# Attention by single tiles against attention by steps of two tiles: transposes and scores in groups, AV products in two places per unit

## The chip, the cores and the metric

The kernel runs on one core of a Trainium2 chip. The metric is the device time of one execution in microseconds; before the change three runs gave 1063.75, 1064.16 and 1065.99, so a median of 1064.16. A profiled execution of the same kernel is where all durations come from.

## The reference

Three stages follow each other. The first is attention over q, k, v of 4 batches x 8 heads x 576 positions x 64, with a bias per head made by a small network from the distance of two positions:

```python
scores = scale * np.matmul(q, k.transpose(0, 1, 3, 2))
scores = scores + bias.transpose(2, 0, 1)[None, :, :, :]
scores = scores - np.max(scores, axis=-1, keepdims=True)
attn = np.exp(scores)
attn = attn / (np.sum(attn, axis=-1, keepdims=True) + 1e-09)
return np.matmul(attn, v)
```

The result, as 2304 tokens of 512, goes through a dense layer with a rational activation (512 to 2048 and back), and then through one of eight experts per token (512 to 1024 and back). The change lies in attention and at its seam to the dense layer.

## The kernel before, in words

**The engines.** TensorE (PE) runs all products and transposes, and writes PSUM. VectorE (DVE), ScalarE (ACT) and GpSimd (POOL) run elementwise work, and SyncE (SP) issues nearly all DMAs. Each engine takes its instructions in the order in which the Python program emits them; the schedule is written out by hand. A tile of a pool with `bufs=2` has two buffers taken in turn: the first write of a new tile waits until the readers of the tile that had its buffer are done.

**Units and tiles.** A unit is one batch and one pair of heads: 16 units, `NU`. Each has nine tiles of 128 rows of scores: eight of one head each (tile t < 4 of the first head, 4 to 7 of the second), and a ninth with the last 64 rows of both heads. `ORD` is the order in which they come: head one and head two in turn, then the ninth.

**What a tile goes through.** `scores(g)` (L330): four fp32r products of 128x288 (eight for the ninth tile) into a PSUM tile `sc` of two banks, of which there are two. `rowmax(g)` (L346, VectorE): adds the bias, writes `e`, takes the row minimum of the negative. `expo(g)` (L351, ScalarE): the exponential with the row sum. `recip` (L363, L364 on VectorE, L366 on POOL): reciprocals of the sums of two tiles, spread into `rb`. `trans_pe` (L393): four transposes of `e` into a one-bank PSUM tile `tr`; after every second tile two more (L396, L397) of the last 64 columns and of `rb` into `rem`, an `av` tile. `trans_evac` (L370, ScalarE): copies 512 columns to `aT`, and after four tiles 512 columns of `rem` to `aR`. `rest_pe`, `rest_evac` (L417, L418) do the same for the ninth tile.

**AV.** `av_pe(u, n, c)` (L436) multiplies by V with 64 stationary columns for each of two heads, for query columns 0 to 255 (n = 0) or 256 to 575 (n = 1), chunk c of five; `av_evac` (L445, VectorE) scales into `xs`, and SP stores `xs` to `xT` (L447). A place in this text is an unbroken stretch of AV products on TensorE.

**Beside it, for later.** For the next unit q and k chunks are transposed into stacks: `stack_pe(u, i)` for i = 0 to 4 (L289, L291, L293, L294), into a `tr` tile, and read by `stack_evac` one loop turn later: for i = 1 and 3 by two VectorE passes (L310, L311), for 0 and 2 by ScalarE (L307), for 4 by two VectorE passes (L302, L303) and then ScalarE's `qrem` (L305). `split_q` (POOL) splits q into two parts. `conv(i, part)` converts the dense layer's weights, 32 pieces, two per unit: part 0 loads (L51, L53), 1 (L61, L62), 3 (L67), 4 (L70) and 5 (L76) are VectorE, 2 is ScalarE's Square (L65), 6 and 8 POOL, 7 stores.

**The order.** The loop `for g in range(NG + 6)` (L524) takes one tile g per turn: exponentials of g - 2, what is pending from the last turn, transposes of g - 4 (`LAG`), scores of g, stack transposes, row maximum of g - 1, AV products of the previous unit. The tables say in which of a unit's nine turns j the rest comes:

```python
CONV = {0: [(6, -1), (8, -1), (1, 0), (2, 0)], 1: [(3, 0), (7, -1), (0, 1)], 2: [(4, 0)], 3: [(5, 0)], 4: [(6, 0)],
        5: [(1, 1), (8, 0)], 6: [(7, 0), (3, 1), (2, 1), (0, 2)], 7: [(4, 1)], 8: [(5, 1)]}
STACK = {0: 4, 1: 0, 2: 1, 3: 2, 7: 3}
SPLIT = {6: (0,), 7: (1,), 8: (2, 3)}
AV0 = {0: (0, 1), 1: (2,), 2: (3, 4)}
AV1 = {4: (0, 1), 6: (2,), 7: (3,), 8: (4,)}
```

**The seam.** `first_x`, `first_split` and `first_mm` (L449 to L477) run the first three chunks of the dense layer's first product (L671) among the last turns of attention, and `Rational` its activation. The dense layer's second product (L759) needs the weights `w_b`, loaded by `load_wo` (L688), which SP issues after the last `xT` store.

**PSUM.** Eight banks: two `sc` tiles of two banks, two `tr` and two `av` of one.

Of the kernel before, what the change touches and what calls it, by code (L numbers as in the profile page):

```python
# [22 lines left out]
P = 128  # L23
# [65 lines left out]
def attention(ctx, tc, k, ins):  # L89
# [115 lines left out]
    NG = 9 * NU  # L205
    ORD = (0, 4, 1, 5, 2, 6, 3, 7, 8)
    LAG = 4
# [72 lines left out]
    def stack_pe(u, i):  # L280
# [3 lines left out]
        ps = pst.tile([P, 512], F32, name="tr")  # L284
# [73 lines left out]
    def recip(g):  # L358

        n = 1 if g % 9 == 8 else 2  # L360
        if g % 9 % 2 or n == 1:
            st = tiles[g][4]
            nc.vector.tensor_scalar(st[:, 2, 0:n], st[:, 1, 0:n], 1e-9, None, ALU.add)  # L363
            nc.vector.reciprocal(st[:, 3, 0:n], st[:, 2, 0:n])  # L364
            rb = recips[g] = ap.tile([P, 2, D], F32, name="rb")
            nc.gpsimd.tensor_scalar(rb, st[:, 3, 0:n].unsqueeze(2).to_broadcast([P, 2, D]), 1.0, 1.0, ALU.mult, ALU.mult)  # L366
# [8 lines left out]
    def trans_pe(g):  # L375
        u, j = divmod(g, 9)
        t = ORD[j]
        r = units[u]
        both = tiles[g][3]
        if j == 0:  # L380
            r.aT = [None, None]
            r.aR = [None, None]
            r.rem = [None, None]
        if j in (0, 4):
            w = Q1 if j == 0 else S - Q1
            n = j // 4
            r.aT[n] = ap.tile([P, 2, 4, w], F32, name=f"aT{n}", bufs=1)
            r.aR[n] = ap.tile([P, 2, w], F32, name=f"aR{n}", bufs=1)
            r.rem[n] = pst.tile([P, 512], F32, name="av")
        ps = r.tps = pst.tile([P, 512], F32, name="tr")  # L390
        for c in range(4):
            e0 = c // 2 * 2 * P + (640 if 4 <= t < 8 else 0)
            nc.tensor.transpose(ps[:, c * P:(c + 1) * P], both[:, e0 + c % 2:e0 + 2 * P:2], k.idf)  # L393
        if j % 2:
            n, q0 = t % 4 // 2, t % 2 * P
            nc.tensor.transpose(r.rem[n][:, Q1 + q0:Q1 + q0 + P], both[:, 512:640], k.idf)  # L396
            nc.tensor.transpose(r.rem[n][:, q0:q0 + P], recips.pop(g).rearrange("p a n -> p (a n)"), k.idf)  # L397

    def trans_evac(g):
        u, j = divmod(g, 9)  # L400
        t = ORD[j]
        r = units[u]
        pv = r.tps.rearrange("p (c n) -> p c n", c=4)
        if t < 8:
            hd, n, q0 = t // 4, t % 4 // 2, t % 2 * P
            evac("A", r.aT[n][:, hd, :, q0:q0 + P], pv)
            if j in (3, 7):
                evac("A", r.aR[n][:, :, 0:Q1], r.rem[n].rearrange("p (a n) -> p a n", a=2))
        else:
            evac("A", r.aT[1][:, :, :, Q1:Q1 + 64], r.tps.rearrange("p (c h n) -> p h c n", c=4, h=2))  # L410
        if t < 8:
            tiles.pop(g)

    def rest_pe(g):
        both = tiles.pop(g)[3]
        av0, rb = units[g // 9].av0, recips.pop(g)
        nc.tensor.transpose(av0[:, 384:512], both[:, 512:640], k.idf)  # L417
        nc.tensor.transpose(av0[:, 256:384], rb.rearrange("p a n -> p (a n)"), k.idf)  # L418

    def rest_evac(g):  # L420
        r = units[g // 9]
        for hd in range(2):
            ls = slice(64 * hd, 64 * hd + 64)
            evac("A", r.aR[1][ls, :, Q1:Q1 + 64], r.av0[ls, 256:512].rearrange("p (a n) -> p a n", a=2)[:, :, 64 * hd:64 * hd + 64])

    def av_pe(u, n, c):
        r = units[u]
        w = Q1 if n == 0 else S - Q1
        if c == 0:
            r.av = pst.tile([P, 512], F32, name="av")  # L430
            if n == 0:
                r.av0 = r.av
# [53 lines left out]
    for s in range(37):  # L486
        if s == 24:
            conv(0, 0)
# [1068 lines left out]
```

## Time and profile before

| | before |
|---|---|
| runs | 1063.75, 1064.16, 1065.99 us (median 1064.16) |
| the profiled execution's own time | 1065.21 us |
| its span | 1063.4 us |
| TensorE busy, products / weight loads | 1018.1 us (96%) / 885.9 us (83%) |
| VectorE busy | 749.7 us (70%) |
| ScalarE busy | 650.2 us (61%) |
| POOL busy | 277.0 us (26%) |

The span is the time from the first to the last instruction of the profiled execution. Busy shares are means over stages: until about 63 us the bias is made, until about 397 us attention runs, then the dense layer and the experts. A row of a timeline has start, duration, engine, line of the kernel, operation, tiles as out<-in, shapes and a count of merged instructions; in brackets the idle time of the engine before it and what ended it. On TensorE instructions overlap, so the time that one takes from the others is read from start to start.

### The profile page before, as it was taken

What the parts mean: (1) busy time and instruction counts of PE and PEld (TensorE: products, weight loads), DVE (VectorE), ACT (ScalarE), POOL (GpSimd) and SP (SyncE); (2) the same over time, 40 slices, a digit from 0 to 9 for tenths busy, and PEclk for the clock granted to TensorE, in tenths of its full rate; (3) what the DMA queues carried; (4) which work ended last, traced back from release to release, by engine and by line L of the source; (5) the groups of instructions that cost most, each with busy time, mean ns of one, the idle gap of its engine ahead of it and who ended that gap; (6) DMA issues with size and microseconds to landing.
All of it is one profiled execution on the core that took longest, in us unless ns stands there. A gap on an engine that the chain in (4) does not pass through costs nothing. (4 is left out here: it accounts for less than half of the span.)

```text
span 1063.4 us, 19125 instructions
## 1 busy us (share of the span) xinstructions
PE 1018.1 (96%) x6804; PEld 885.9 (83%) x6804; DVE 749.7 (70%) x1544; ACT 650.2 (61%) x1283; POOL 277.0 (26%) x449
## 2 busy tenths in 40 slices
PE   6889999999999999999999999999997899999995
PEld 4667777777777779999999999999996789999983
DVE  7988898888888858888888988988885412111210
ACT  6878788888878856676667666666664322222221
POOL 3434344343343310202103012021041533211210
PEclk9999999999999999999999999999998999999998
DMA  5885885784664327005103121051240356411100
GB/s 166 290 277 159 235 250 171 214 236 118 189 185 116 99 74 296 30 1 23 38 1 31 30 21 40 1 30 60 81 80 1 24 159 215 141 42 40 51 31 18
DMA packets 122072, 113.34 MB, mean 107 GB/s; under 512 B 65055, under 2 KB 94495, under 8 KB 121952
## 3 DMA queue, kind: packets, MB, share of 16 engines
q1 hardware_dynamic: 117828, 101.53, 35.8%
q0 software_dynamic: 3728, 10.25, 3.2%
q8 instruction: 61, 1.00, 0.4%
q14 instruction: 59, 0.48, 0.2%
q10 hardware_dynamic: 396, 0.08, 0.0%
HBM read 78.09 MB, written 33.79 MB: 105 GB/s over the span
## 5 line engine op out<-in xcount | busy, mean ns | idle before, releaser
L759 PE MATMUL sc<-gh,w_b 128*128 128x384 f32 x752 | 208.8, 339 | 1.3 <-ACT x L766 1.3
L759 PEld LDWEIGHTS sc<-gh,w_b 128*128 128x128 f32 x752 | 138.6, 189 | 2.2 <-ACT x L766 1.9
L759 PE MATMUL sc<-gl,w_b 128*128 128x384 f32 x376 | 127.1, 338 | 0.0
L393 PEld LDWEIGHTS tr<-idf,e 128*128 128x128 f32 x576 | 80.5, 207 | 49.2 <-issue 25.0
L351 ACT ACTIVATE e<-e,st 128x576 f32<-128x576 f32 x144 | 112.2, 779 | 12.2 <-DVE st L346 10.3
L370 ACT COPY aT<-tr 128x512 f32<-128x512 f32 x144 | 84.5, 587 | 45.8 <-PE tr L393 44.0
L346 DVE CUSTOM_DVE_ANT_0 e<-sc,bias_s 128x576 f32<-128x576 f32 x144 | 107.7, 749 | 5.1 <-PE sc L330 4.0
L1086 DVE SCALAR_TENSOR_TENSOR hl<-tr,hh 128x256 fp32r<-128x256 f32 x56 | 23.8, 425 | 121.4 <-ACT hh L1085 119.5
L671 PE MATMUL tr<-kn,w_a 128*128 128x384 f32 x372 | 107.1, 342 | 0.1
L393 PE MATMUL tr<-idf,e 128*128 128x128 f32 x576 | 104.6, 304 | 1.7 <-DVE kk L311 0.9
L330 PE MATMUL sc<-kk,qS 128*128 128x288 f32 x512 | 99.1, 315 | 0.7 <-DVE st L346 0.7
L660 ACT CAST gh<-t 128x768 fp32r<-128x768 f32 x47 | 39.3, 836 | 86.2 <-DVE t L656 86.2
L436 PE MATMUL av<-aT,vn 128*64 128x320 f32 (+1 forms) x512 | 82.8, 424 | 0.0
L1076 PE MATMUL tr<-kn,w_a 128*128 128x256 f32 x448 | 81.4, 280 | 0.9 <-issue 0.9
L330 PEld LDWEIGHTS sc<-kk,qS 128*128 128x128 f32 x512 | 72.9, 191 | 2.2 <-DVE st L346 1.0
L1076 PEld LDWEIGHTS tr<-kn,w_a 128*128 128x128 f32 x448 | 69.7, 188 | 1.8 <-issue 1.5
L759 PEld LDWEIGHTS sc<-gl,w_b 128*128 128x128 f32 x376 | 71.1, 189 | 0.0
L1097 PE MATMUL sc<-w_a,hh 128*128 128x512 f32 x224 | 70.9, 393 | 0.0
L671 PEld LDWEIGHTS tr<-kn,w_a 128*128 128x128 f32 x372 | 68.0, 188 | 2.9 <-issue 2.3
L366 POOL TENSOR_SCALAR rb<-st 128x128 f32<-128x128 f32 x80 | 23.8, 298 | 170.4 <-DVE st L364 154.3
L863 POOL DMA_INDIRECT tab<-ids,si x18 | 21.2, 1180 | 174.4 <-DVE cum L859 168.1
L654 DVE SCALAR_TENSOR_TENSOR t<-t,coef,r 128x768 f32<-128x768 f32 x47 | 47.7, 1016 | 24.2 <-ACT r L650 24.2
(305 smaller groups left out, 2531.1 us busy)
## 6 DMA issues: line engine op xcount, KB each, us to landing
bias_d<-bo SPq DMA_DIRECT2D x36, 295.5 KB, 3.6
kn<-in_k_dram SPq DMA_DIRECT2D x64, 128.0 KB, 3.6
cst<-in_moe_w_out_dram SPq DMA_DIRECT2D x16, 512.0 KB, 4.4
wo_d<-cvw SPq DMA_DIRECT2D x16, 512.0 KB, 2.8
cst<-in_moe_w_in_dram SPq DMA_DIRECT2D x16, 512.0 KB, 4.5
w_b<-wo_d SPq DMA_DIRECT2D x16, 512.0 KB, 6.2
w_b<-in_moe_w_dram SPq DMA_DIRECT2D x16, 512.0 KB, 7.6
x_d<-xr SPq DMA_DIRECT2D x18, 256.5 KB
```

The source lines that it names most:

```text
L330: nc.tensor.matmul(ps[:, hf, 0:HF], st, mv[:, hf * HF:(hf + 1) * HF], start=n == 0, stop=n == last)
L346: nc.vector.tensor_tensor_reduce(out=ev, in0=ps[:, :, 0:HF], in1=bv, scale=-1.0, scalar=3.0e38, op0=ALU.add, op1=ALU.min, accum_out=st[:, ...
L351: nc.scalar.activation(e, e, AF.Exp, bias=st[:, 0:1], scale=-1.0, accum_out=st[:, 1:2])
L370: nc.scalar.copy(dst, src)
L393: nc.tensor.transpose(ps[:, c * P:(c + 1) * P], both[:, e0 + c % 2:e0 + 2 * P:2], k.idf)
L436: nc.tensor.matmul(r.av[64 * hd:64 * hd + 64, 0:w], st, mv, start=c == 0, stop=c == 4)
L654: nc.vector.scalar_tensor_tensor(q.t, q.t, co[:, 0:1], q.r, ALU.add, ALU.mult)
L660: self.nc.scalar.copy(gh, q.t)
L671: nc.tensor.matmul(h[:, 0:k.NB], k.wi[f][:, wv, dc * P:(dc + 1) * P], xv[dc], start=n == 0, stop=n == 11)
L759: nc.tensor.matmul(r.acc[dc][:, 0:NB], wo[f][:, wv, ws], gv, start=f == 0 and n == 0, stop=f == NF - 1 and n == 2)
L1076: nc.tensor.matmul(ps[:, 0:n], w[:, wv, cs], xv[dc // 2][:, dc % 2], start=j == 0, stop=j == 11)
L1097: nc.tensor.matmul(r.acc[a], r.h[f][hv][:, cs], wa[8 + f][:, wv], start=f == 0 and n == 0, stop=f == 7 and n == 2)
```

## The change

The loop goes by steps of two tiles: five steps q = 0 to 4 per unit (four pairs and the ninth tile alone), `NS = 5 * NU`. In a step TensorE runs the transposes of the pair two steps back, all eight into one two-bank tile `tp` (one buffer), the two transposes of the remainder and of `rb` into a `rem` tile, and then the scores of both tiles. ScalarE copies the eight transposes at once (1024 columns) and the remainder in 256 columns each. `expo` of a pair's second tile comes in the step after. AV products stand in q = 0 (all of n = 0) and q = 2 (all of n = 1). The stack transposes move from `tr` tiles to `av` tiles; `rem` is an `av` tile of every step. Conversion, stack, split and load tables are new, and the first conversion load moves from step 24 of the bias stage to step 0 of attention. The `tr` tiles of the later stages come from a pool of their own (`trp`), which replaces `tp` at the seam. PSUM: two `sc` tiles of two banks, `tp` two banks, two `av`.

```diff
-    NG = 9 * NU
+    NS = 5 * NU
-    LAG = 4
@@ stack_pe
-        ps = pst.tile([P, 512], F32, name="tr")
+        ps = pst.tile([P, 512], F32, name="av")
...
+    def recip(u, q):
+        n = 1 if q == 4 else 2
+        st = tiles[9 * u + 2 * q][4]
...
+    def trans_pe(u, q):
         r = units[u]
+        both = tiles[9 * u + 2 * q][3]
...
+        r.tps = trp.tile([P, 2, 512], F32, name="tp", bufs=1)
+        for hd in range(2 if q < 4 else 1):
+            for c in range(4):
+                e0 = c // 2 * 2 * P + 640 * hd
+                nc.tensor.transpose(r.tps[:, hd, c * P:(c + 1) * P], both[:, e0 + c % 2:e0 + 2 * P:2], k.idf)
+        r.rem = pst.tile([P, 512], F32, name="av")
+        nc.tensor.transpose(r.rem[:, P:2 * P], both[:, 512:640], k.idf)
+        nc.tensor.transpose(r.rem[:, 0:P], recips.pop((u, q)).rearrange("p a n -> p (a n)"), k.idf)
+
+    def trans_evac(u, q):
         r = units[u]
+        n, q0 = q // 2, q % 2 * P
+        rem = r.rem[:, 0:2 * P].rearrange("p (a n) -> p a n", a=2)
+        if q < 4:
+            evac("A", r.aT[n][:, :, :, q0:q0 + P], r.tps.rearrange("p h (c n) -> p h c n", c=4))
+            evac("A", r.aR[n][:, :, q0:q0 + P], rem)
...
@@ the loop
-        if s == 24:
-            conv(0, 0)
...
+    CONV = {0: [(3, -1)], 1: [(4, -1), (5, -1), (6, -1), (8, -1)], 2: [(1, 0), (2, 0), (3, 0)], 3: [(4, 0), (5, 0), (6, 0), (8, 0)],
+            4: [(1, 1), (2, 1)]}
+    MOVE = {0: [(0, 0)], 2: [(7, -1), (0, 1)], 4: [(7, 0)]}
+    LOAD = {0: (0, 1), 1: (2, 3), 2: (4, 5)}
+    STACK = {1: (4, 0), 3: (1, 2), 4: (3,)}
+    SPLIT = {0: (-1, (3,)), 3: (0, (0,)), 4: (0, (1, 2))}
...
+    for s in range(NS + 3):
+        u, q = divmod(s, 5)
...
         for f in pend:
             f()
         pend = []
+        for part, d in CONV.get(q, ()):
+            if 0 <= 2 * u + d < 32:
+                conv(2 * u + d, part)
+        before, two = divmod(s - 1, 5), divmod(s - 2, 5)
+        if 1 <= s <= NS and before[1] < 4:
+            expo(9 * before[0] + 2 * before[1] + 1)
+        if 2 <= s < NS + 2:
+            trans_pe(*two)
+            trans_evac(*two)
+        if s < NS:
+            for g in pair(u, q):
+                scores(g)
+        if 1 <= s <= NS:
+            recip(*before)
+        if u + 1 < NU:
+            for i in STACK.get(q, ()):
+                ps = stack_pe(u + 1, i)
+                pend.append(lambda u=u, i=i, ps=ps: stack_evac(u + 1, i, ps))
+        if s < NS:
+            for g in pair(u, q):
+                rowmax(g)
+            expo(9 * u + 2 * q)
+        if q in (0, 2) and 0 <= last < NU:
+            for c in range(5):
+                av_pe(last, q // 2, c)
+            pend.append(lambda u=last, n=q // 2: av_evac(u, n))
+        for part, d in MOVE.get(q, ()):
+            if 0 <= 2 * u + d < 32:
+                conv(2 * u + d, part)
...
+        if NS <= s < NS + 2:
+            first_mm(x0, s - NS)
...
+        if s == NS + 2:
+            first_mm(x0, 2)
...
     for f in pend:
         f()
+    for t in sorted(later):
+        if t >= NS + 3:
+            later[t]()
```

## Rows read from the trace of the kernel before

**Rows 1.** Windows, 200 to 300 us: busy time (and instructions) by engine, clock, DMA

```profile
core 0: us, PE busy (x) PEld busy (x) DVE busy (x) ACT busy (x) POOL busy (x), PEclk, DMA share, GB/s
200.00:300.00 100.00, 100.00 (x736) 76.51 (x734) 86.10 (x234) 80.71 (x182) 40.79 (x77) 1.00 0.66 185
```

**Rows 2.** Timeline of PE over one unit: start, duration, engine, line, tiles, count

```profile
299.98 1.08 PE L436 MATMUL av<-aT,vn 128*64 128x256 f32 x8
300.99 0.75 PE L393 MATMUL tr<-idf,e 128*128 128x128 f32 x4
...
302.50 0.65 PE L436 MATMUL av<-aT,vn 128*64 128x256 f32 x4
303.08 0.74 PE L393 MATMUL tr<-idf,e 128*128 128x128 f32 x4
...
305.95 0.74 PE L393 MATMUL tr<-idf,e 128*128 128x128 f32 x4
306.45 0.77 PE L330 MATMUL sc<-kk,qS 128*128 128x288 f32 x4
...
310.69 0.78 PE L330 MATMUL sc<-kk,qS 128*128 128x288 f32 x4
311.31 0.63 PE L393 MATMUL tr<-idf,e 128*128 128x128 f32 x4
311.69 0.77 PE L330 MATMUL sc<-kk,qS 128*128 128x288 f32 x4
312.39 0.76 PE L436 MATMUL av<-aT,vn 128*64 128x320 f32 x4
...
319.66 1.08 PE L436 MATMUL av<-aT,vn 128*64 128x256 f32 x8
```

**Rows 3.** The page's costliest groups, ScalarE: busy, mean ns of one | idle before

```profile
L351 ACT ACTIVATE e<-e,st 128x576 f32<-128x576 f32 x144 | 112.2, 779 | 12.2 <-DVE st L346 10.3
L370 ACT COPY aT<-tr 128x512 f32<-128x512 f32 x144 | 84.5, 587 | 45.8 <-PE tr L393 44.0
```

**Rows 4.** Timeline of DVE, 285.3 to 288.4 us

```profile
285.36 0.69 DVE L310 CAST kk<-tr 128x512 fp32r<-128x512 f32 x1 [0.68 <-PE tr L291]
286.09 0.69 DVE L311 TENSOR_TENSOR kk<-tr,kk 128x512 fp32r<-128x512 f32 x1
286.70 0.41 DVE L445 TENSOR_TENSOR xs<-av,aR 128x256 f32<-128x256 f32 x1
287.03 0.75 DVE L346 CUSTOM_DVE_ANT_0 e<-sc,bias_s 128x576 f32<-128x576 f32 x1
...
287.70 0.42 DVE L76 CAST w_a<-cvt 128x512 fp32r<-128x512 f32 x1
...
288.31 0.74 DVE L346 CUSTOM_DVE_ANT_0 e<-sc,bias_s 128x576 f32<-128x576 f32 x1
```

**Rows 5.** Timeline of all engines: stack 4 is read by DVE, then by ACT

```profile
300.96 0.27 DVE L302 CAST kk<-tr 128x128 fp32r<-128x128 f32 x1
...
301.64 0.27 ACT L305 CAST qrem<-tr 128x128 fp32r<-128x128 f32 x1 [0.54 <-DVE kk L303]
```

**Rows 6.** Instructions of the tile cst: count, duration ns min/median/max, first and last start us

```profile
L62 DVE SCALAR_TENSOR_TENSOR cvt<-cst,cvt x32: 691/693/1106, 62.3 to 368.1; 128x512 uint32<-128x512 uint32 x32
```

**Rows 7.** Waits of PE over the span: us in total, times, longest

```profile
PE tr L289 <- ACT qrem L305: 1.5, 3, 0.5
```

**Rows 8.** Timelines of SP, DVE and PE at the start of attention

```profile
69.11 0.52 SPq L51 DMA_DIRECT2D cst<-in_moe_w_out_dram  x1
...
73.75 0.43 DVE L61 TENSOR_SCALAR cvt<-cst 128x512 uint32<-128x512 uint32 x1 [1.63 <-DMA cst<-in_moe_w_out_dram]
...
80.34 0.80 PE L330 MATMUL sc<-kk,qS 128*128 128x288 f32 x4 [0.29 <-DVE st L346]
```

**Rows 9.** Timelines of PE and SP at the end of attention

```profile
373.47 1.30 PE L330 MATMUL sc<-kk,qrem 128*128 128x288 f32 x8
376.08 17.07 SPq L447 DMA_DIRECT2D xT<-xs  x2
397.49 0.77 PE L759 MATMUL sc<-kn,w_b 128*128 128x384 f32 x3 [1.36 <-ACT kn L660]
```

More of the change, by code (lines that the diff above doesn't have):

```diff
@@ L356, in attention @@
     recips = {}
[L358 to L366, printed above, removed]
+    def recip(u, q):
+        n = 1 if q == 4 else 2
+        st = tiles[9 * u + 2 * q][4]
+        nc.vector.tensor_scalar(st[:, 2, 0:n], st[:, 1, 0:n], 1e-9, None, ALU.add)
+        nc.vector.reciprocal(st[:, 3, 0:n], st[:, 2, 0:n])
+        rb = recips[u, q] = ap.tile([P, 2, D], F32, name="rb")
+        nc.gpsimd.tensor_scalar(rb, st[:, 3, 0:n].unsqueeze(2).to_broadcast([P, 2, D]), 1.0, 1.0, ALU.mult, ALU.mult)
     def evac(eng, dst, src):
@@ L372, in evac @@
             nc.vector.tensor_copy(dst, src)
-    def trans_pe(g):
-        u, j = divmod(g, 9)
-        t = ORD[j]
+    def trans_pe(u, q):
         r = units[u]
[L379 to L386, printed above, removed]
+        both = tiles[9 * u + 2 * q][3]
+        n = q // 2 if q < 4 else 1
+        if q in (0, 2):
+            w = Q1 if q == 0 else S - Q1
+            if q == 0:
+                r.aT = [None, None]
+                r.aR = [None, None]
@@ new lines, in attention @@
+    x0 = None
+    for s in range(NS + 3):
+        u, q = divmod(s, 5)
+        last = u - 1
+        if u + 2 < NU:
+            for i in LOAD.get(q, ()):
+                load_unit(u + 2, i)
+        if 2 <= u < NU and q == 1:
+            load_v(u)
+        if u + 2 < NU and u % B == 2 and q in (1, 3):
+            load_bias(u // B + 1, q // 2)
+        if u % B == B - 1 and u + 1 < NU and q >= 2:
+            load_bias(u // B + 1, 2 * q - 2)
+            load_bias(u // B + 1, 2 * q - 1)
+        if u and u < NU and u % B == 0 and q == 0:
+            load_bias(u // B, 8)
+        if s == 1:
@@ L537, in attention @@
             load_bias(0, 8)
-        if 12 <= g < 21 or g in (28, 30, 32, 34, 36):
+        for _ in range(setups.count(s)):
             next(setup)
-        if g in later:
-            later[g]()
-        if 0 <= g - 3 < NG:
-            recip(g - 3)
-        if 0 <= g - 2 < NG:
-            expo(g - 2)
+        if s in later:
+            later[s]()
         for f in pend:
@@ new lines, in attention @@
+        for part, d in MOVE.get(q, ()):
+            if 0 <= 2 * u + d < 32:
+                conv(2 * u + d, part)
+        if q in SPLIT:
+            d, parts = SPLIT[q]
+            if 2 <= u + 2 + d < NU:
+                for i in parts:
+                    split_q(u + 2 + d, i)
+        if s == NS - 4:
+            x0 = first_x()
+        if NS - 3 <= s <= NS:
+            first_split(x0, s - (NS - 3))
+        if NS <= s < NS + 2:
+            first_mm(x0, s - NS)
+        if s == NS + 1:
+            tctx.close()
+            k.trp = k.persist.enter_context(tc.tile_pool(name="trp", bufs=2, space=PSUM))
```

124 lines of the change are left out of this document (22 added, 102 removed).

## The prediction

> **What bounds the kernel now.** I read the windows first. In a steady 100 us of attention TensorE shows 100.00 us busy, VectorE 86.10, ScalarE 80.71, at full granted clock [rows 1]: TensorE sets the pace, and VectorE has 14% to spare. Then TensorE's timeline over one unit [rows 2]. The first AV product of a unit starts at 299.98 and its successor at 319.66: a unit takes 19.68 us, and there is no idle stretch in it. What can be saved is in the joints. Four transposes that follow scores reach the next score after 0.38 us (311.31 to 311.69); behind AV products they need 0.50 (305.95 to 306.45). Four scores hand over to transposes after 0.62 us (310.69 to 311.31), to AV products after 0.70 (311.69 to 312.39). A place with one AV chunk takes 0.58 us (302.50 to 303.08), one with two 1.01 (299.98 to 300.99): a chunk costs 0.43, the place 0.15 more. So every place of AV products costs 0.08 + 0.15 + 0.12 = **0.35 us** beyond its products. A unit has seven such places, AV0 three and AV1 four, of which the rows show some.
>
> The Trainium skill, page "TensorEngine Tiling (Array Packing)", section "Key Properties", gives a rule that bears on this: a change of tiling mode, not merely of tile, drains TensorE. AV products use 64 columns, all else 128, and the rows agree, with 0.35 us a place.
>
> **The change part by part.**
>
> *AV in two places per unit, not seven.* Five places fewer: 5 x 0.35 = **-1.75 us** a unit on TensorE, so 17.93. The products themselves stay.
>
> *Ten transposes, then eight scores.* The counts stay (46 transposes, 40 scores per unit). A turn from transposes to scores costs next to nothing: 0.38 + 0.62 = 1.00 us for eight instructions [rows 2], 0.125 each. Zero, between 0 and 0.1 us a unit.
>
> *One copy of transposed chunks.* Two copies of 512 columns at 0.587 us each [rows 3] become one of 1024. Two rows of ScalarE bound it: at best it is 0.1 us shorter than two, at worst as long. I take 1.02, estimated from the same row with its per-column time doubled. The two 512-column aR copies become four of 256. Together some 0.3 us a unit less on ScalarE, which is not the bound: zero.
>
> *PSUM buffers.* Here I expect the price. Stack transposes move from the tag `tr` to `av`; the reciprocal and remainder tile (`rem`) now takes an `av` buffer in every step. The two `av` buffers go round twelve tiles per unit in this order: rem(3), AV0 in q=0; rem(4), stack 4, stack 0 in q=1; rem(0), AV1 in q=2; rem(1), stack 1, stack 2 in q=3; rem(2), stack 3 in q=4. Each tile waits until the one two earlier has been copied out, and TensorE is in order, so eight scores queue behind a waiting `rem`. Two are late.
>
> - rem(0) waits for stack 4. From TensorE's first transpose after AV0: av_evac starts on VectorE at 0.15 (the AV row ends 0.07 after the next transpose starts [rows 2]; the hand-off is an estimate) and takes 0.33 (286.70 to 287.03 [rows 4]); conversion part 4 0.72, since part 5 reads its result (a pass of 0.69 and a hand-off of 0.03, as from 285.36 to 286.09); part 5 and the reciprocals 0.61 (287.70 to 288.31); two row minima 2 x 0.67 (287.03 to 287.70); then the stack's two VectorE passes up to qrem's start 0.68 (300.96 to 301.64 [rows 5]), qrem itself 0.27 and 0.05: 4.15 us. TensorE meanwhile has 14 transposes at about 0.12, eight scores at 0.13, six stack transposes at 0.07 (most of them short) and the 0.12 behind AV: 3.28. **Wait 0.87.**
> - rem(2) waits for stack 1. From the first transpose after AV1 the ten transposes take 1.2 and four scores 0.78 to their end [rows 2], so VectorE has work at 2.0, and has done with the part of its queue that stands before it; row minima to 3.35; CAST 0.73 and subtract 0.69 [rows 4] to 4.77, and 0.05. TensorE arrives after 18 transposes at 0.12, eight scores at 0.13, eight stack transposes at 0.09 and the 0.12, at 4.06. **Wait 0.75.**
>
> The trace of before has this wait in small: TensorE L289 sat 1.5 us in three places until qrem was read out of the buffer it was to overwrite [rows 7]. The other tiles come free in time (stack 2 and stack 3 by 0.05 to 0.1 us). Bounds for the two waits together: 1.62 if every hand-off is as above; 1.0 if VectorE is free 0.3 us earlier each time, 2.4 if POOL or a DMA delays its conversions by 0.4. I take 1.65.
>
> The same tiling page, section "PSUM Bottleneck", speaks against the change: tiling speeds TensorE up, not the emptying of PSUM, which may become the limit. The wait of [rows 7] agrees; by it the saving above would not arrive whole.
>
> So a steady unit is 17.93 + 1.65 = 19.58 against 19.68: **-0.1**, and for the 14 units 1 to 14 -1.4 us.
>
> *First conversion load.* It moves from bias step 24 into step 0, behind four loads of unit 2 on SP's queue. There a load issued at 69.11 today is first used at 73.75, and VectorE sat 1.63 us for it [rows 8]; the new first load has the same four loads ahead, so it lands at about the same time. But now conversion parts 1 to 3 of unit 0 stand in step 2 on VectorE and ScalarE (the Square), ahead of the exponential, the chunk copy and the row minima. Chain: 73.75; Square 0.6 (as a copy of 512), exponential 0.78 [rows 3], chunk copy 1.02 bring ScalarE to 76.2, until when the transposes of step 3 wait. VectorE: conversion 1.8, reciprocals 0.3, minima 1.35, next conversion 1.06, exponential awaited 0.4, reciprocals 0.3, minima 1.35, stack 1.42: stack 1 is read by 81.4, and only then rem(2), eight scores, four stack and ten transposes (3.0) follow. Unit 1's first score comes at 84.4, not 80.34 [rows 8]: **+4.1**, between +1 (a load that lands 3 us sooner) and +6.
>
> *The end.* Unit 15 stacks nothing, so it has no such wait and keeps four places' saving, -1.4. Behind its last scores (373.47) today 24.0 us pass to the first product of the next stage (397.49) [rows 9]. That product needs w_b, whose load stands on SP behind the last xT store: SP is in L447 from 376.08 for 17.07 us, to 393.15. In the new order last scores 1.1, transposes 1.7, first product chunk 2.1, AV0 2.3, transposes 1.0, chunk 2.1 come to 10.3; the activation chain starts when ScalarE has copied the last transposes, at 9.3: eight ScalarE passes of about 0.5 with VectorE's between them, then the quotient's three VectorE passes and av_evac at 0.6, and the store, to 16.4 (all estimates by size). From the store's end on the load takes 4.3 (393.15 to 397.49): 20.7. **-3.3.** TensorE's own work ends at 19.8, so the load decides. Bounds 0 and -5.
>
> Other moved DMAs (xT stores one step later, v and bias loads on whole steps) are issued more than a step ahead of use; cover is gone only if SP falls some 3 us behind.
>
> Sum: -1.4 + 4.1 - 1.4 - 3.3 = **-2.0 us**, of which I keep -1 because the setup instructions in units 1 and 3 come on top of the two waiting chains. The profiled execution took 1065.21 us (span 1063.4), 1.05 above the median of 1064.16; so 1064.2 for such an execution, **1063** as a median.
>
> **Rivals.**
>
> A, *the buffers come free in time*: then TensorE alone decides, 14 x 1.65 = 23 us less, 1040; with half the wait 1051. For: TensorE has 100.00 us in 100 today, so 1.75 us a unit must show if nothing follows. Against: the sums 4.15 against 3.28 need VectorE faster by a fifth. The rule of "Key Properties" taken alone gives this time.
>
> B, *the waits outgrow the saving*: the break-even lies at 1.75 us of waits per unit. VectorE's instructions between av_evac and the stack copy go into the wait one for one. Conversion pass L62 takes 0.693 at the median and 1.106 at most [rows 6], so such instructions do stretch when they meet other work; 0.3 us at each of the two places gives 2.25, +0.5 x 14 = +7 us, 1070; with a late conversion load as well 1075. For: VectorE has 86.10 of 100 and would have 93% of a 17.9 us unit. Against: the long ones stand outside the two chains.
>
> C, *TensorE takes the AV products as dearly as now* (the place price sits in the chunk, not in the switch): +1.65 a unit remains, 1085. Against: one-chunk and two-chunk places differ by exactly a chunk.
>
> **How the numbers follow.** 0.2% (2.1 us) is about what a measurement of this kernel can tell from no change. Forecast case 0.50, own range 1057 to 1068; A 0.23 (1037 to 1055), B 0.25 (1067 to 1077), C 0.02. Of the forecast case 0.27 lies within 0.2%, 0.17 faster, 0.06 slower; A is faster; B is slower but for 0.02; C slower. Faster 0.40, same 0.29, slower 0.31. The range leaves out the lower half of A and the upper end of B with C: **1050 to 1073**.
>
> **What would show it.** Right: L436 in two groups per unit with some 5.2 us of wall time; TensorE idle before `rem` transposes for about 0.9 us in q=2 (until qrem, L305) and 0.75 in q=4 (until kk, L311), a unit near 19.6; TensorE without work for 4 to 5 us at 71 to 76; the w_b product near 4.5 us after the last av_evac. Wrong: units near 18 us with TensorE never idle (A), waits of over 1 us each or VectorE without gaps (B), a first unit of less than 17 us, or a long idle elsewhere.

## The result and the profile after

The changed kernel takes **1071.39 us** (median of 15 runs, 1067.87 to 1075.09) against 1065.08 for the kernel before (15 runs, 1063.20 to 1066.81): ratio **1.0062**, 95% interval 1.0051 to 1.0072. It is 0.6% slower. The forecast was 1063, with faster the likeliest of the three. The profiled execution of the changed kernel is the slowest of its 15 (1075.09, span 1073.2), so the two profiles differ by 9.8 us where the medians differ by 6.3: what follows explains the profiled pair.

The window of [rows 1], now of the changed kernel (busy time and count by engine, clock, DMA):

```profile
200.00:300.00 100.00, 92.04 (x700) 76.11 (x696) 82.96 (x225) 75.67 (x165) 40.77 (x74) 0.98 0.62 180
```

TensorE was busy 100.00 of 100 before; now 8 us are idle (2.8 of them one long wait in unit 7, told below), and the other engines are no busier than before. So TensorE waits, and for nobody who is full. One steady unit of the changed kernel, from TensorE's timeline, answers to [rows 2] (start, duration, engine, line, tiles, count; in brackets the idle time before it and who ended it):

```profile
258.34 1.20 PE L389 MATMUL tp<-idf,e 128*128 128x128 f32 x8
260.23 0.33 PE L391 MATMUL av<-idf,e 128*128 128x128 f32 x1 [0.69 <-ACT qrem L305]
260.40 0.27 PE L392 MATMUL av<-idf,rb 128*128 128x128 f32 x1
260.43 1.30 PE L330 MATMUL sc<-kk,qS 128*128 128x288 f32 x8
261.66 2.38 PE L420 MATMUL av<-aT,vn 128*64 128x320 f32 x16
263.86 0.71 PE L420 MATMUL av<-aR,vrem 128*64 128x320 f32 x4
264.50 1.23 PE L389 MATMUL tp<-idf,e 128*128 128x128 f32 x8
...
267.57 1.19 PE L389 MATMUL tp<-idf,e 128*128 128x128 f32 x8
268.92 0.33 PE L391 MATMUL av<-idf,e 128*128 128x128 f32 x1 [0.16 <-ACT qS L307]
...
270.26 0.60 PE L291 MATMUL av<-idf,kn 128*128 128x128 f32 x4
271.15 1.23 PE L389 MATMUL tp<-idf,e 128*128 128x128 f32 x8 [0.29 <-ACT aT L369]
```

Three waits stand in it. The bracket counts from the modelled end of the instruction before; by the distance of the starts they cost 0.86, 0.32 and 0.45 us, 1.63 together. The first is rem(0), which waits until `qrem` has been copied out of stack 4's buffer; the kernel before had waits for the same copy, 1.5 us in its whole run [rows 7]. The second is rem(2), let go by ScalarE's L307, so it waits for stack 2 and not, as forecast, for stack 1. (That copy ends at 268.87, VectorE's last pass over stack 1 at 269.39; so the two `av` buffers are not always taken in turn.) The third was not forecast: the transposes of step 0 wait for the single `tp` buffer to be copied.

All waits of TensorE in the attention part, 63 to 385 us (us in total, times, longest):

```profile
PE av L391 <- ACT qrem L305: 12.1, 15, 1.7
PE tp L389 <- ACT aT L369: 9.5, 15, 5.5
PE av L391 <- ACT qS L307: 3.9, 3, 2.8
```

The longest wait of each line is two to nine times its mean: beside the steady waits there are single **stands** (long waits that occur once), in units 0, 2, 3 and 7. Unit by unit (from a unit's first score to the next one's, in us, read off the timelines) they are easy to see:

| unit | 0 | 1 | 2 | 3 | 4 | 5, 6 | 7 | 8 to 14 |
|---|---|---|---|---|---|---|---|---|
| before | 16.44 | 20.49 | 19.68 | 20.39 | 20.45 | 19.68 | 19.68 | 19.68 |
| after | 22.96 | 19.82 | 20.69 | 22.94 | 19.87 | 19.8 | 23.51 | 19.9 |

So of the 9.8 us between the profiles unit 0 makes 6.5; units 1 to 14 7.9, of which 0.21 x 14 = 2.9 is the steady unit and 5 the stands (some 7.5 in units 2, 3 and 7, less the 2.3 by which units 1, 3 and 4 of the kernel before exceeded its steady 19.68); unit 15 and the tail give 3.2 back, the start 0.8 and the stages behind 0.6. The largest stand is at the start. ScalarE's timeline shows its cause, TensorE's its size, as in [rows 8]:

```profile
69.14 0.63 ACT L307 CAST qS<-av 128x512 fp32r<-128x512 f32 x1
73.90 0.68 ACT L65 ACTIVATE cvq<-cst 128x512 f32<-128x512 f32 x1 [4.13 <-DMA cst<-in_moe_w_out_dram]
74.48 0.76 ACT L351 ACTIVATE e<-e,st 128x576 f32<-128x576 f32 x1
...
75.24 0.99 ACT L369 COPY aT<-tp 128x1024 f32<-128x1024 f32 x1
```

```profile
69.49 1.30 PE L330 MATMUL sc<-kk,qS 128*128 128x288 f32 x8
76.28 1.98 PE L389 MATMUL tp<-idf,e 128*128 128x128 f32 x8 [5.49 <-ACT aT L369]
```

The conversion's Square sits 4.13 us at the head of ScalarE's queue until its load lands; the exponential and the copy of the transposed chunks stand behind it, and TensorE behind the copy. The stand in unit 7 also begins with a transfer of the conversion. VectorE's timeline:

```profile
221.59 0.68 DVE L70 SCALAR_TENSOR_TENSOR cvt<-cvq,cvt 128x512 f32<-128x512 f32 x1
225.22 0.43 DVE L76 CAST cvw<-cvt 128x512 fp32r<-128x512 f32 x1 [2.95 <-DMA wo_d<-cvw]
```

VectorE's waits from 100 to 240 us show one more of this kind, 1.1 us in unit 2 (at 120.25), and none in unit 3:

```profile
DVE cvw L76 <- DMA wo_d<-cvw: 4.0, 2, 2.9
```

SP's queue around the wait in unit 7:

```profile
218.75 1.48 SPq L220 DMA_DIRECT2D bias_s<-bias_d  x3
220.33 0.37 SPq L83 DMA_DIRECT2D wo_d<-cvw  x1
220.81 0.37 SPq L51 DMA_DIRECT2D cst<-in_moe_w_out_dram  x1
221.23 3.90 SPq L220 DMA_DIRECT2D bias_s<-bias_d  x6
```

The store that empties the one `cvw` buffer was issued at 220.33, behind three bias transfers and ahead of six; VectorE wants the buffer at 222.3 and gets it at 225.2. The row minima and the stack's copies are behind it. The bias loads alone make no stand: in unit 11 the same nine go out, at a time when the conversion no longer stores, and the unit takes 19.9 us:

```profile
300.69 2.52 SPq L220 DMA_DIRECT2D bias_s<-bias_d  x3
303.32 0.38 SPq L53 DMA_DIRECT2D cst<-in_moe_w_in_dram  x1
303.75 2.87 SPq L220 DMA_DIRECT2D bias_s<-bias_d  x6
```

Around such a stand the clock falls too. Three stretches (columns as in [rows 1]):

```profile
71.50:81.70 10.20, 5.42 (x26) 5.40 (x27) 6.50 (x18) 6.26 (x13) 2.62 (x5) 0.50 0.65 190
136.40:139.80 3.40, 3.40 (x16) 2.23 (x16) 2.84 (x10) 3.35 (x9) 0.30 (x1) 0.50 0.82 207
228.60:231.90 3.30, 3.30 (x16) 3.29 (x16) 2.62 (x7) 2.56 (x6) 0.30 (x1) 0.50 0.81 306
```

A granted clock of 0.50 is the lower of the two levels, 1.2 GHz: some 10 us of it around the 5.49 us stand, 3.4 us each after those of 1.67 (unit 3) and 2.80 us (unit 7). In unit 3 eight scores and the AV products behind them take 5.00 us (136.12 to 141.12) against 3.43 at the full clock (260.43 to 263.86), so the low clock costs 1.6 us there. In unit 0 it costs 2.4: from the transposes at 76.28 to those at 81.73 pass 5.45 us, and 3.07 for the same instructions above (264.50 to 267.57).

At the end, against [rows 9], unit 15 takes 14.76 us to its last scores (15.32 before), and from there to the next stage's first product pass 21.38 us (24.02 before).

### The profile page after: what moved, and what is told of

Its sections match the earlier page's. It is cut to its first block, busy times and chain, and to the rows that moved or that the text cites. A ratio compares the mean times of both kernels' runs of the same rounds, so it can differ in the third digit from the quotient of the medians.

```text
span 1073.2 us, 19047 instructions
## 1 busy us (share of the span) xinstructions
PE 1004.8 (94%) x6804; PEld 894.9 (83%) x6804; DVE 750.6 (70%) x1544; ACT 646.5 (60%) x1251; POOL 278.3 (26%) x449
## 5 line engine op out<-in xcount | busy, mean ns | idle before, releaser
L346 DVE CUSTOM_DVE_ANT_0 e<-sc,bias_s 128x576 f32<-128x576 f32 x144 | 103.8, 753 | 5.3 <-PE sc L330 4.6
L389 PE MATMUL tp<-idf,e 128*128 128x128 f32 x576 | 90.3, 298 | 10.6 <-ACT aT L369 10.6
L389 PEld LDWEIGHTS tp<-idf,e 128*128 128x128 f32 x576 | 76.4, 209 | 27.6 <-ACT aT L369 14.4
L369 ACT COPY aT<-tp 128x1024 f32<-128x1024 f32 (+1 forms) x80 | 74.1, 926 | 27.7 <-PE tp L389 26.8
L330 PE MATMUL sc<-kk,qS 128*128 128x288 f32 x512 | 85.9, 310 | 0.5 <-ACT bo L187 0.2
L420 PE MATMUL av<-aT,vn 128*64 128x320 f32 (+1 forms) x512 | 70.0, 416 | 0.0
L640 ACT ACTIVATE r<-q,one 128x768 f32<-128x768 f32 x47 | 44.1, 938 | 33.2 <-DVE q L636 33.2
```

Of the source, the lines that this page charges most:

```text
L330: nc.tensor.matmul(ps[:, hf, 0:HF], st, mv[:, hf * HF:(hf + 1) * HF], start=n == 0, stop=n == last)
L346: nc.vector.tensor_tensor_reduce(out=ev, in0=ps[:, :, 0:HF], in1=bv, scale=-1.0, scalar=3.0e38, op0=ALU.add, op1=ALU.min, accum_out=st[:, ...
L369: nc.scalar.copy(dst, src)
L389: nc.tensor.transpose(r.tps[:, hd, c * P:(c + 1) * P], both[:, e0 + c % 2:e0 + 2 * P:2], k.idf)
L420: nc.tensor.matmul(r.av[64 * hd:64 * hd + 64, 0:w], st, mv, start=c == 0, stop=c == 4)
L640: nc.scalar.activation(q.r, q.q, AF.Ln, bias=self.one[:, 0:1], scale=1.0)
```

## The experiments

All ratios are against the kernel before, timed on the same chip in the same session. The changed kernel's own is 1.0062.

**First load back (e1).**

```diff
+        if s == 24:
+            conv(0, 0)
```

(and no load in step 0 of unit 0)

> The changed kernel with the first conversion load alone put back into step 24 of the bias stage. Theory: the 5.5 us in which TensorE stands at 70.8 us, and the half clock behind it, come from that load arriving late, so unit 0 (first score to first score of unit 1, 22.96 us in the changed kernel, 16.44 before) goes back to 16 to 18 us and the run is 4 to 6.5 us shorter than the changed kernel, about 1066. Rival: the wait is one of ScalarE's own order (copies behind stack copies in the new step), and the load only happens to stand in it: unit 0 stays at 22 to 23 us and the time within 1 us of the changed kernel.

Measured: 1073.87 us, 1.0065 (1.0046 to 1.0085): nothing gained. Unit 0 took 21.13 us. Its 5.49 us stand is gone; another of 2.58 us stands ten microseconds later, and ScalarE's timeline of this run shows what is late:

```profile
77.93 0.61 ACT L307 CAST qS<-av 128x512 fp32r<-128x512 f32 x1
80.72 0.68 ACT L65 ACTIVATE cvq<-cst 128x512 f32<-128x512 f32 x1 [2.18 <-DMA cst<-in_moe_w_out_dram]
```

It is the *second* chunk's load, issued at 75.78 behind unit 2's loads on SP. The theory was right that TensorE waits for a conversion load, wrong in taking it for a matter of the first load alone.

**Two buffers for the converted chunk (e2).**

```diff
-                c.w = k.cv.tile([P, 2, 512], F32R, name="cvw", bufs=1)
+                c.w = k.cv.tile([P, 2, 512], F32R, name="cvw", bufs=2)
```

> The changed kernel with a second buffer for the converted weights (cvw). Theory: the two single stands of TensorE (1.67 us at 134, 2.80 us at 225, each followed by 3.4 us of half clock) come from VectorE waiting in line 76 for the store of the part before, which lies behind the bias loads on SP's queue: with a second buffer line 76 waits no more, units 3 and 7 take 20 to 20.5 us instead of 22.9 and 23.5, and the run is 4 to 7 us shorter. Rival: the bias loads themselves, or the routing set-up on VectorE (0.8 us of small operations at 134), make TensorE stand: then both stands remain and the time is within 1 us of the changed kernel. In between: the one at 225 goes, the one at 134 stays, 3 to 4 us.

Measured: 1071.29 us, 1.0048 (1.0035 to 1.0061). Units 3 and 7 fell from 22.94 and 23.51 to 21.11 and 21.17, and VectorE no longer waits in L76. What is left in unit 7 is 1.57 us of TensorE, because now the load is late:

```profile
221.41 0.61 ACT L307 CAST qS<-av 128x512 fp32r<-128x512 f32 x1
223.16 0.71 ACT L65 ACTIVATE cvq<-cst 128x512 f32<-128x512 f32 x1 [1.14 <-DMA cst<-in_moe_w_out_dram]
```

In unit 7 the store was the first cause, the load stood close behind it. In unit 3, where L76 had not waited, TensorE still stands 1.37 us (1.67 in the changed kernel), but the low clock behind it is gone. The median gained less than the units did, and less than the 4 to 7 us expected; the intervals leave 0 to 0.3% of gain over the changed kernel.

**Square moved (e3).**

```diff
-    CONV = {0: [(3, -1)], 1: [(4, -1), (5, -1), (6, -1), (8, -1)], 2: [(1, 0), (2, 0), (3, 0)], 3: [(4, 0), (5, 0), (6, 0), (8, 0)],
-            4: [(1, 1), (2, 1)]}
+    CONV = {0: [(2, -1), (3, -1)], 1: [(4, -1), (5, -1), (6, -1), (8, -1)], 2: [(1, 0), (2, 0), (3, 0)], 3: [(4, 0), (5, 0), (6, 0), (8, 0)],
+            4: [(1, 1)]}
```

> The changed kernel with one Square of the conversion (part 2 of the second weight chunk of a unit) moved on ScalarE from step 4 to step 0 of the next unit. Theory: the 0.45 us that the transposes of step 0 wait for the one tp buffer is the queue of ScalarE ahead of the copy aT (stack copy, Square 0.68, exponential): without the Square the copy ends 0.68 earlier, the wait goes, the steady unit falls from 19.89 to 19.3 to 19.45 us, and the run is 6 to 9 us shorter (1062 to 1065). Rival: the next wait, for the remainder's buffer or for the row minima's score buffer, lies close behind: steady unit 19.75 to 19.9, 0 to 2 us.

Measured: steady unit 19.55 us, as near the theory as its rival is far; the `tp` wait is gone from it. The run: 1072.37, 1.0049 (1.0035 to 1.0063), far from 1062 to 1065: unit 7 stood even longer (23.81), and what the steady units gained was hardly to be seen in the time.

**Stacks copied early (e4).**

```diff
-    STACK = {1: (4, 0), 3: (1, 2), 4: (3,)}
+    EARLY = {1: 0, 3: 2}
+    STACK = {1: (4,), 3: (1,), 4: (3,)}
...
+        if u + 1 < NU and q in EARLY:
+            stack_evac(u + 1, EARLY[q], stack_pe(u + 1, EARLY[q]))
         if s < NS:
             for g in pair(u, q):
                 scores(g)
```

(and stack 0 instead of stack 4 is the first of a unit's stacks)

> The changed kernel with stacks 0 and 2 transposed ahead of the scores of steps 1 and 3 and copied by ScalarE at once, ahead of the exponential, instead of at the start of the next step; the remainder of step 2 then stands behind stack 0 or finds its buffer free. Theory: the waits of the remainders (0.86 us in step 2, 0.32 in step 4) are waits for the late stack copies, and go: the steady unit falls from 19.89 to 18.5 to 18.9 us, the run by 14 to 20 us (1051 to 1057). Rival: the wait passes to the next one (the remainder takes the other stack's buffer, which VectorE leaves at 269.4, or the exponential, 0.65 us later, makes the next transposes wait): steady unit 19.5 or more, at most 6 us.

Measured: steady unit 19.04 us, 1068.19 us, 1.0014 (1.0003 to 1.0025). Both waits for `rem` are gone from the steady unit; what is left in it is the `tp` wait, 0.50 us in the bracket instead of 0.29. Between the theory (18.5 to 18.9) and its rival: the waits were what they were taken for, and part of the gain went into the next one. The time is far from the 1051 to 1057 expected, because the stands remain (unit 0 22.83, unit 2 22.22, unit 7 23.78).

**The conversion fed in time (f1).** Two `cst` and two `cvw` buffers, ten bias buffers, and

```diff
-    MOVE = {0: [(0, 0)], 2: [(7, -1), (0, 1)], 4: [(7, 0)]}
+    MOVE = {0: [(0, 1)], 2: [(7, -1), (0, 2)], 4: [(7, 0)]}
```

with the first load in the bias stage and the bias loads issued behind MOVE.

> The changed kernel with the feed of the conversion alone changed: two buffers each for the loaded (cst) and the converted (cvw) chunk, every load one chunk earlier (the first in the bias stage), the bias loads behind the conversion's transfers in SP's order, with ten bias buffers instead of eleven. Theory: what the single stands of units 0, 2, 3 and 7 share is a conversion transfer that lands after ScalarE or VectorE asks for it (at 80.6 us in the run with only the first load moved, at 223.1 in the run with two cvw). Then units 1 to 14 all take 19.8 to 20.0 us, unit 0 17 to 18, first mm2 at 396 to 399 us, the run 6 to 9 us below the changed kernel (1062 to 1066). Rival: the stands are made by the traffic itself (288 KB bias loads, store and loads on the same DMA engines), which stays: one other transfer, a unit's q or k or the bias, is late instead, units 3 and 7 stay above 21 us and the gain is under 3 us.

Measured: 1065.10 us, **0.9988** (0.9978 to 0.9998), 0.7% below the changed kernel. Unit 0 16.89, units 2 and 7 19.9, first mm2 (the start of the dense layer's second product) at 397.39 us. Only unit 3 kept 21.02. This is the test of the cause: the buffers, the early loads and SP's order are changed and nothing of the step's own order, the steady unit stays at 19.9, and the whole loss is gone.

**More places (f2).**

```diff
+        if q in (0, 2) and 0 <= last < NU:
+            for c in range(2):
+                av_pe(last, q // 2, c)
         if s < NS:
             for g in pair(u, q):
                 scores(g)
...
-            for c in range(5):
+            for c in range(2, 5):
```

> The changed kernel with each half's second products cut in two again: two of five chunks ahead of the scores of the same step, three behind them, so four places per unit instead of two; nothing else moves. Theory: a place costs TensorE 0.35 us beyond its products wherever it stands, so the steady unit rises from 19.89 to 20.5 to 20.6 us and the run by 9 to 11 us (1080 to 1083). Rival: the steady unit holds 1.6 us of waits that take up what TensorE gains or loses: the longer steps give ScalarE and VectorE more time before the remainder and the transposes, the waits shrink, the unit rises by under 0.3 us and the run by under 4 us.

Measured: 1088.20 us, 1.0203 (1.0183 to 1.0223), steady unit 21.05: 1.16 us for two places, 0.58 each. The waits absorbed nothing: rem(0)'s stays 0.86. (By the chain of the prediction it begins with the copy of the AV products and moves along with them; that is a reading, not a test.) The price is above 0.35 because of where the new place lies, behind a transpose. The last transpose ahead of scores takes 0.03 us from start to start (260.40 to 260.43 above); ahead of AV products it takes 0.56 and 0.38:

```profile
256.41 0.27 PE L392 MATMUL av<-idf,rb 128*128 128x128 f32 x1
256.97 1.08 PE L420 MATMUL av<-aT,vn 128*64 128x256 f32 x8 [0.28 <-PE av L392]
...
265.08 0.27 PE L392 MATMUL av<-idf,rb 128*128 128x128 f32 x1
265.46 1.30 PE L420 MATMUL av<-aT,vn 128*64 128x320 f32 x8
```

**Steady fixes and feed together (f3, f4).** f3 is e3, e4, two `cst` buffers with early loads and the late bias loads; f4 is e3, e4 and f1.

> The changed kernel with the Square in step 0, stacks 0 and 2 copied early by ScalarE, two cst buffers with every load one chunk earlier, and the bias loads behind the conversion's transfers (one cvw buffer as in the changed kernel). Theory: the gains add, since each takes away a wait of its own: steady unit 19.89 - 0.85 - 0.45 = 18.5 to 18.7 us, first mm2 at 375 to 382 us, the run 1042 to 1050, below both kernels. Rival: with TensorE faster VectorE (17.0 us busy per unit, 16.97 in the changed kernel) becomes the bound through the row minima, the steady unit stays at 18.9 to 19.1 us and the run at 1053 to 1058.

> As the run before it, and with two cvw buffers and ten bias buffers. Theory: units 3 and 7 no longer wait for the store in line 76, which a 2 to 3 us stand each would have cost, so 2 to 6 us below the run before it: 1040 to 1047. Rival: with the bias loads behind the store it lands in time with one buffer too: the same time within 2 us.

Measured: f3 1056.62 us, 0.9907 (0.9890 to 0.9923), f4 **1054.89**, 0.9895 (0.9879 to 0.9912), both below both kernels. The steady unit is 19.03 in either: the rival of f3 was right that it stays near 19, and the time lies in its range. All of e3's gain is gone when e4 is there. TensorE's timeline of f4 shows the new place:

```profile
252.97 1.26 PE L330 MATMUL sc<-kk,qS 128*128 128x288 f32 x6
254.42 0.53 PE L330 MATMUL sc<-kk,qS 128*128 128x288 f32 x2 [0.20 <-DVE kk L311]
254.88 1.95 PE L420 MATMUL av<-aT,vn 128*64 128x256 f32 x16
```

Eight scores take 1.91 us to the next product instead of 1.23 (260.43 to 261.66 above): the second tile reads the key stack that VectorE has only just written. The expectation of f4 itself came out as its rival: 1.7 us below f3, which the two intervals do not tell from nothing.

**The part alone in the kernel before (g1).**

```diff
-    AV0 = {0: (0, 1), 1: (2,), 2: (3, 4)}
-    AV1 = {4: (0, 1), 6: (2,), 7: (3,), 8: (4,)}
+    AV0 = {2: (0, 1, 2, 3, 4)}
+    AV1 = {7: (0, 1, 2, 3, 4)}
...
-            if j == 8:
+            if j == 7:
```

> The kernel before, with its second products in two places per unit instead of seven (all five chunks of the first half in tile 2, all of the second in tile 7) and nothing else of the change. Theory: each place costs 0.35 us beyond its products and TensorE has no waits to absorb it, so the steady unit falls from 19.68 to 17.9 to 18.3 us and the run by 18 to 26 us (1040 to 1048), which makes this part of the change the gain and the regrouping the loss. Rival: the rest of the order needs the slack: with all chunks in one place the next tile's transposes or scores wait for ScalarE's copies or VectorE's minima, the steady unit stays above 19.2 us and the run gains under 7 us.

Measured: 1076.77 us, **1.0104** (1.0089 to 1.0119), steady unit 20.30. The theory falls, clearly. TensorE's waits of the attention part have grown:

```profile
PE tr L289 <- ACT qrem L305: 16.9, 14, 1.9
PE tr L393 <- ACT qS L307: 7.1, 15, 0.7
```

The first was 1.5 us in three places before [rows 7]. TensorE's timeline shows both in one unit, and one joint without a wait:

```profile
289.01 0.69 PE L393 MATMUL tr<-idf,e 128*128 128x128 f32 x4
289.46 0.77 PE L330 MATMUL sc<-kk,qS 128*128 128x288 f32 x4
291.35 0.54 PE L289 MATMUL tr<-idr,qs 128*128 128x128 f32 x4 [1.12 <-ACT qrem L305]
...
298.14 0.77 PE L330 MATMUL sc<-kk,qS 128*128 128x288 f32 x4
299.37 0.75 PE L393 MATMUL tr<-idf,e 128*128 128x128 f32 x4 [0.45 <-ACT qS L307]
```

Four scores take 0.62 us to the next instruction where nothing waits (310.69 to 311.31 in [rows 2]); here it is 1.89 and 1.23, so the two waits cost 1.27 and 0.61 us, 1.88 a unit. Without them the unit would be 20.30 - 1.88 = 18.42: five places fewer save TensorE 1.26 us, **0.25 each and not 0.35**, and the waits take more than that away. The seven places had not only cost TensorE time; they had stood where it would otherwise have waited.

**The one copy undone (g2).**

```diff
-        r.tps = trp.tile([P, 2, 512], F32, name="tp", bufs=1)
+        r.tps = []
         for hd in range(2 if q < 4 else 1):
+            r.tps.append(trp.tile([P, 512], F32, name="tp", bufs=2))
...
+            for hd in range(2):
+                evac("A", r.aT[n][:, hd, :, q0:q0 + P], r.tps[hd].rearrange("p (c n) -> p c n", c=4))
```

> The changed kernel with the one two-bank buffer tp and its one copy of 1024 columns undone: two buffers of one bank, one copy of 512 columns for each tile of a step, as in the kernel before. Theory: the transposes of step 0 wait 0.45 us because the single buffer is free only after the whole copy (0.99 us); with two the first tile's is free half a copy earlier, so that wait falls to 0 to 0.1 us; but four more copies per unit cost ScalarE some 0.1 us each (two of 0.55 for one of 0.99). Steady unit 19.4 to 19.6 us, the run 4 to 8 us below the changed kernel. Rival: ScalarE's queue, not the buffer, sets the wait: the copy ends later by what the second one costs, and the unit stays at 19.8 to 20.0 us.

Measured: steady unit **19.55** as the theory said, 1073.27 us (1.0064, 1.0041 to 1.0086) not: units 3 and 7, with their stands, took 24.39 and 22.95. Two copies of 512 columns take 1.05 to 1.08 us back to back, the one copy 0.99 to 1.02. So that part of the change saves ScalarE 0.06 us a step and costs TensorE 0.34 us a unit.

**What VectorE does late (g3, g4).** g3 is f4 with L61 and L62 of the second chunk in step 0 instead of step 4; g4 has in addition

```diff
+                if i == 3:
+                    nc.scalar.copy(units[u + 1].kH[:, 640:1152], ps)
```

and no L310 for this stack on VectorE.

> The best kernel so far (f4, 1054.9 us) with both first VectorE operations of the second weight chunk (lines 61 and 62, 1.1 us) moved from step 4 to step 0 of the next unit. Theory: of its steady unit of 19.03 us some 0.7 is the second score tile of step 0, which waits for VectorE's two operations on stack 3 (ended 254.365, score at 254.42); 1.1 us ahead of them gone, that wait goes: 18.3 to 18.5 us, the run 7 to 10 us shorter (1045 to 1048). Rival: VectorE's work as a whole (17.0 us per unit) paces the unit and the wait only moves to step 0 or 1, where the row minima come later: 18.8 to 19.1 us, under 3 us.

> As the run before it, and with the first operation on stack 3 (the rounding copy of 128x512) made by ScalarE at once instead of by VectorE at the start of the next step, which takes 0.69 us per unit off VectorE and puts as much on ScalarE. Theory: if the run before still waits on VectorE, 0.2 to 0.5 us per unit less, 1040 to 1047. Rival: ScalarE, at 15.7 us per unit, delays the copy aT or the exponential of tile 8 by as much, and TensorE waits for the transposes: same or slower than the run before it.

Measured: g3 1060.52 us, 0.9953 (0.9939 to 0.9966), *slower* than f4, steady unit 19.71: the wait moved to step 1, where TensorE's timeline has

```profile
261.70 0.33 PE L392 MATMUL av<-idf,rb 128*128 128x128 f32 x1
262.69 0.55 PE L289 MATMUL av<-idr,qs 128*128 128x128 f32 x4 [0.66 <-DVE xs L429]
```

because VectorE comes later to the copy of AV0, whose buffer the early stack takes. That neither the theory nor its rival foresaw the loss has a reason in VectorE's timeline of g3:

```profile
257.74 0.90 DVE L61 TENSOR_SCALAR cvt<-cst 128x512 uint32<-128x512 uint32 x1
258.68 1.24 DVE L62 SCALAR_TENSOR_TENSOR cvt<-cst,cvt 128x512 uint32<-128x512 uint32 x1
```

The two moved passes take 2.1 us in step 0, not the 1.1 they took in step 4: POOL runs its part of `split_q` (L265, L268) in the same microseconds, from 257.68 to 259.36. So the move put 1 us a unit on VectorE. g4: **1047.67**, 0.9829 (0.9811 to 0.9848), steady unit 18.59. With 0.69 us off VectorE's queue the profile names no wait of the steady unit any more (L61 and L62 are back at 0.42 and 0.69 us, but for unit 3; L67 behind them takes 1.03 where it took 0.69).

**Routing set-up (h1).**

```diff
-    setups = [g * 5 // 9 for g in (*range(12, 21), 28, 30, 32, 34, 36)]
+    setups = [6, 7, 7, 8, 8, 9, 10, 10, 11, 28, 33, 38, 43, 48]
```

> The best run (g4, 1047.7 us) with the five last parts of the routing set-up moved from steps 15 to 20 (unit 3) to steps 28, 33, 38, 43 and 48, one per unit, each in a unit's fourth step. Theory: VectorE's queue in unit 3 is what makes the stack's transposes wait 1.44 us for the second products' evacuation, so unit 3 falls from 20.32 to 18.6 to 18.8 us, units 5 to 9 rise by at most 0.1 each, and the run is 1.0 to 1.8 us shorter (about 1046). Rival: the unit's traffic makes VectorE late (its first two conversion operations took 0.89 and 1.23 us there instead of 0.42 and 0.69): unit 3 stays above 19.5 us and the time the same within 1 us.

Measured: **1045.64 us, 0.9819** (0.9804 to 0.9833); unit 3 18.58. It was VectorE's queue: the bias loads still run in unit 3, and the two passes that took 0.89 and 1.23 us there take 0.42 and 0.69. The unit shows it; the ratio, 0.1% below g4's, lies within both intervals. This is the best version of the study, 1.8% below the kernel before. Its window of 200 to 300 us:

```profile
200.00:300.00 100.00, 100.00 (x777) 81.99 (x776) 91.32 (x249) 86.07 (x190) 45.78 (x80) 1.00 0.71 199
```

TensorE is full again, with 777 instructions where [rows 1] has 736.

## Why the prediction was wrong

Two steps failed. The first is the sentence "Other moved DMAs [...] are issued more than a step ahead of use; cover is gone only if SP falls some 3 us behind." It put all transfers but the first conversion load and the `w_b` load at nothing, in one line and without a row for any of them; the conversion's stores and its later loads are not even named. The runs showed in its place: with one `cvw` buffer VectorE waited for the conversion's store, 1.1 us in unit 2 and 2.9 us in unit 7, there with three bias loads ahead of it on SP's queue and six behind; with one `cst` buffer the next load stood close behind (e1, e2). The stands in units 2, 3 and 7, with the low clock behind two of them, made 5 us of the 9.8. (Unit 3's own stand is mostly VectorE's queue with the routing set-up, which h1 takes away; for the set-up the prediction had kept 1 us, and f1, with the feed mended, leaves 1.1.) With the feed mended the same step order takes 1065.10, 1.2 us below the kernel before in its session. That the forecast was 1.2 below as well is luck: f1 has no late first load (+4.1 in the sum, +0.5 in f1), its steady unit is 0.3 us longer than the forecast one, and the sum took 19.68 for all units of before, where units 1, 3 and 4 took 20.4 to 20.5.

The second is "So every place of AV products costs 0.08 + 0.15 + 0.12 = 0.35 us". It was read at places behind scores and taken for all seven; it made the steady unit 0.3 us too short, 4.3 us in 14 units.

The terms one by one:

- *AV in two places, -1.75.* Mis-sized: **-1.4**. The steady unit of the changed kernel without its waits is 19.89 - 1.63 = 18.26 us, against 19.68; g1, with the same two places and no other part of the change, gives 18.42, -1.26. Four of the seven places stood behind stack transposes, not behind scores. There four transposes need 0.45 us to the next score without any AV products (289.01 to 289.46 in g1), where they need 0.38 behind scores and 0.50 behind AV products: less is saved than the 0.12 of the sum.
- *Ten transposes, then eight scores: zero, at most 0.1.* Right in the main, by the same two numbers: 18.26 us in the order by steps, 18.42 by tiles. A turn's last transpose takes 0.03 to 0.04 us to the score where others take 0.12, so four turns fewer lose four cheap transposes; but eight scores in a row take 1.15 us (265.70 to 266.85) and twice four 1.24, which gives the same back.
- *One copy of transposed chunks, 1.02.* Measured 0.99 to 1.02. But two copies of 0.587 less 0.1 are 1.07, so the number lay below the working's own bounds: right by luck. g2 shows that it matters little for ScalarE.
- *rem(0), 0.87.* Measured 0.86. *rem(2), 0.75:* measured 0.32, and for another buffer: the trace has TensorE go on at stack 2's copy, 0.5 us before VectorE has read stack 1. The strict order of two tiles back, which the text on the kernel before states too, was an assumption; why the pool chose otherwise was not tried.
- *"The other tiles come free in time."* Not `tp`: 0.45 us a unit. e3 and g2 both take it away (19.55).
- So the waits summed to 1.63 against 1.65 forecast, one error cancelling the other, which is luck again. The steady unit is 19.68 - 1.42 + 1.63 = 19.89 us against 19.58: +0.21 where -0.1 was forecast.
- *First conversion load, +4.1, bounds 1 to 6.* Unit 0 grew by 6.5. The chain was right (load, Square, exponential, copy, transposes; they go on at 76.28, forecast 76.2), but the half clock behind the stand, 2.4 us, was no term of the sum, and e1 shows that with the first load early the second is late.
- *Unit 15, -1.4, and the end, -3.3.* Measured -0.6 and -2.6. The end's chain is right: the w_b load goes out at 403.51, 0.4 us behind the store at 403.08, and its first product runs at 407.91. Unit 15 saves four places, some 1 us at the price measured in g1, and loses 0.5 where TensorE waits for POOL's `rb` (378.77).

Rival B named the outcome, 1070 to 1075 "with a late conversion load as well". Both halves happened, the first in another way than it says: the waits came out as forecast, 1.63, but the saving they had to outgrow was 1.42 and not 1.75. The prediction's own sign of being wrong, "a long idle elsewhere", is the stand in unit 7. The doubt of [rows 7] was the better guide of the two rules weighed against the trace: g1 shows that fewer AV places do save TensorE time (1.26 us a unit) and that the saving does not arrive by itself. By the Trainium skill, page "TensorEngine Tiling (Array Packing)", section "Key Properties", a change of tiling mode drains TensorE, and section "PSUM Bottleneck" of the same page warns that the emptying of PSUM may become the limit; g1's waits are for copies out of PSUM (L305 16.9 us, L307 7.1). No run here separates such a drain from the rest of what a place costs.

That stack copies (e4), `tp` (e3, g2) and the feed (f1) are the causes is shown by runs that take each away. Not tried: which of the three parts of the feed matters most in f1. Only argued from the rows: why a place behind stack transposes saves less.

## What to carry to other kernels

A place that costs an engine time may be the cover of a wait. Before you price its removal, ask what TensorE would meet next if it came there that much sooner, and check the order of every queue at that moment; here the price was paid in waits for copies two engines away. Transfers that move need a row each: for every one, when the queue reaches it, when it lands, which instruction asks for it, and what stands behind that instruction. When several waits lie close together, the fix of one shows the next, so test them together as well as alone (e1, e2 and e3 gained nothing to 0.14% each in the time; the version that holds them all, with e4, the feed of f1, g3, g4 and h1, is 2.4% below the changed kernel). And when an operation is moved, look at what runs beside it in its new place: in g3 it took twice as long there.

## What the runs showed of the hardware

- The last transpose ahead of a score product takes TensorE 0.03 to 0.04 us from start to start, one ahead of another transpose 0.12, one ahead of AV products 0.38 and 0.56 (f2). Eight score products in a row take 1.15 us, twice four 1.24.
- A place of AV products costs by its neighbours: 0.35 us between scores and transposes [rows 2], 0.25 on average over the five places taken away in g1, 0.58 over the two added in f2, which stand between a transpose and scores.
- TensorE's clock falls to the lower level for 3.4 us behind some single stands (1.67 and 2.80 us in the changed kernel, 2.58 in e1, 2.31 in f4) and not behind others of the same length (1.57 in e2, 2.95 in e1, 2.31 in g4).
- Two conversion passes on VectorE, 0.42 and 0.69 us elsewhere, took 0.90 and 1.24 us in step 0 of g3, and 0.89 and 1.23 in unit 3 of g4, while POOL ran L265 and L268; at the same place of h1, where they came earlier, they took 0.42 and 0.69.
